# Three edits of order in a state-space and memory-attention kernel: V in four tiles, scalings before products on VectorE, the end of the third segment over more rounds

## The chip, the cores and the metric

The kernel runs on one core of one Trainium2 chip. That core has five engines that matter here: TensorE (PE in the profile, with its weight loads as PEld), VectorE (DVE), ScalarE (ACT), GpSimd (POOL) and SyncE (SP), which issues most of the DMAs. ScalarE and GpSimd also issue a few (ACTq, POOLq). The metric is device time in microseconds (us) from start to end of one launch; lower is better. The profile's own clock, the span, starts at the first recorded instruction.

## The reference

Two branches on the same input are mixed by a gate. `a` is a diagonal state-space layer, whose kernel `K` of length 2048 is built from exponentials and applied as a long convolution by FFT; `b` is attention in four segments of 512 tokens with a memory that is carried from segment to segment. Cut to what matters:

```python
# a: convolution through the spectra
P = exp((A * dt[:, None])[:, :, None] * pos)            # D=448, N=256, L=2048
K = 2.0 * einsum("dn,dnl->dl", C, P).real
y = irfft(rfft(u_t, 2 * L) * rfft(K, 2 * L))[..., :L] + u * D_skip
# b: 16 heads of 28, segments s = 0..3
for s in range(4):
    p = softmax(qs @ ks.T * scale + causal)
    a_dot = p @ vs
    a_mem = (phi(qs) @ M) / (phi(qs) @ z + 1e-6)
    outs.append(g * a_mem + (1 - g) * a_dot)
    M, z = M + phi(ks).T @ vs, z + phi(ks).sum()
b = concat(outs) @ wo
out = gate * a + (1 - gate) * b
```

## The kernel before

The program has a first half (to about 430 us) that builds `K`, transforms the input and projects Q, K and V into DRAM, and a second half, `second_half`, in which all the edits lie. There the work is written out by hand in **units** and **rounds**.

A unit `i` (0 to 15) is one group of four heads, `hg = i % 4`, of one segment, `s = i // 4`. It has six rounds `r` (0 to 5), and one pass of the loop in `second_half` issues one round of many generators, each of which goes on by one step:

- `pair`: the scores of unit `i` (`weigh`: matmuls into the bank `ps_w`, exponential on ScalarE into `PT`, the causal mask on GpSimd), interleaved with the row maxima of unit `i + 2` (`maxima`: mask matmuls and scores into `ps_mx`, then a maximum on VectorE into `mx`). `ps_w` and `ps_mx` have one buffer each, so a round's mask matmuls wait for the maximum of the round before.
- in rounds 0 and 1, the last steps of the maxima of unit `i + 1` (`peak`): a transpose into the bank `ps_m`, a copy `mn`, and a DMA from GpSimd's queue into the Q tile.
- in rounds 0, 1 and 2, `values` of the unit before: the product of `PT` and V into `ps_pv`, key tile 0 in round 0, key tile 1 in round 1, key tiles 2 and 3 and a copy to `pvs` in round 2. So unit 4's round 2 is the last use of segment 0's V, and unit 5's round 0 the first of segment 1's.
- a step of `seg_end`, the end of a segment, if one is under way (`ends`).
- a step of `convolve`: of 16 blocks of the spectra, in turn `transform` (kernel spectrum to `ks`, with a swap of halves by DMA), `product` (input spectrum, and two multiplications `pr` on VectorE), an empty step, and `back` (inverse matmuls into `ps_c`, first half with the first product, second half with the second; copy `bs`, stored to DRAM). It runs in units 1 to 12.

A round to which none of these brings matmuls (`busy` is false) is followed by two or three filler matmuls, `turn_over`.

The engines' orders are fixed: TensorE's and ScalarE's by the program's order, VectorE's in `attend` and `convolve` by `k.dve`, which chains each instruction to the one issued before. The two multiplications of a block are not issued where they arise. `product` puts them on the list `k.later`, and `catch_up` takes them from it: one behind each maximum (line 1053), up to two more after `peak` (line 1404), one at once in rounds 1 and 2 (`k.spread`), and the rest ahead of `back` (line 646). So they stand on VectorE ahead of whatever the segment's end issues in that round.

`seg_end(s)` (line 1221) begins in round 2 of unit 4s + 4 and takes one step to a round, unless the table `STEPS` (line 1460) says more. Its steps:

1. load of four rows of the skip input `xt`; DMA of the softmax denominators out of `pvs` into `dn`, from ScalarE's queue.
2. to 5. four steps `t`, in each of which the recall from memory that an earlier end has prepared (`recall`) scales one head group, `am[hg]`, by a matmul into `ps_m` and one VectorE instruction; in the third, the reciprocal of `dn` (`inverse`) on VectorE, in the fourth its two DMAs.
6. and 7. skip input times gate on ScalarE and times `D_skip` on GpSimd (`scaled`), two tiles a step.
8. to 11. `norm` scales one head group of `pvs` a step: a matmul into `ps_m` (for `s == 2` every second one into `ps_c`), one VectorE instruction, and for `s > 0` a second, which adds `am`.
12. to 19. the projection with `wo`, four tiles of two halves each (`out_mm`, "po"): two head groups to a half, all in `ps_m`; after the second half one VectorE instruction makes `tb`, which goes to DRAM (`TB`). The loads and the reciprocal of the next recall are issued in between.
20. to 23., for `s == 2` only: the four scalings of the last recall, all through `ps_m`.

`STEPS` gives the third segment's end 2, 3, 2 and 2 steps in rounds 2 to 5 of unit 13, and in unit 14 each round has two. `ps_m` has a single buffer, shared by transposes, scalings and projection.

In unit 14 round 2 `join` starts to load the `rest` tiles out of `TB`; from unit 14 round 4 `last` does the final transform of the convolution, in `ps_c` and `ps_mx` by turns, and adds `rest`. Its results go to `out` and, for the last segment, to `YD`, from which `last_end` (line 1270) reads them once more.

V of a segment is one tile, 128 x 4 x 512, with one buffer (`load_v`, line 1100). It is loaded in round 2 of units 4, 8 and 12 (line 1410), behind its last use.

Of the kernel before, what the change touches and what calls it, by code (L numbers as in the profile page):

```python
# [27 lines left out]
SEG = 512  # L28
# [955 lines left out]
def attend(nc, k, ap):  # L984
# [36 lines left out]
    def maxima(i):  # L1021


        q, kk = Q[i], K[i]
        mx = ap.tile([128, 4, 4], F32, tag="mx", name="mx", bufs=2)
        for b, hp in MSTEPS:
            pt = k.ps("mx")
            o, n = DIAGONALS[b]
            for j in range(4):
                for x in range(2):  # L1030
                    h = 2 * hp + x
                    r = slice(32 * h, 32 * h + 32)
                    k.mm(
                        pt[:, x, o : o + n].rearrange("p (b c) -> p b c", c=128)[:, :, 32 * j :],
                        k.mk[r, j, :128],
                        k.mk[r, j, 128 : 128 + n].rearrange("p (b c) -> p b c", c=128)[:, :, 32 * j :],
                        start=(j == 0), stop=True, tile_position=(32 * h, 0), skip_group_check=True,
                    )
            yield
            for t, o, n in PLACES[b]:  # L1040
                qt = 3 - t
                for x in range(2):
                    h = 2 * hp + x
                    r = slice(32 * h, 32 * h + 32)
                    k.mm(
                        pt[:, x, o : o + n], q[r, 0, 128 * qt : 128 * qt + 128], kk[r, 0, :n],
                        start=False, stop=True, tile_position=(32 * h, 0), skip_group_check=True,
                    )
            for t, o, n in PLACES[b]:
                v.tensor_reduce(  # L1050
                    mx[:, 2 * hp : 2 * hp + 2, 3 - t : 4 - t], pt[:, :, o : o + n], AX.X, ALU.max,
                )
            k.catch_up(1)
            yield
        yield
        yield
        pm = k.ps("m")
        k.tr(pm[:16, :128], mx.rearrange("p h t -> p (h t)"), k.ident)
        mn = ap.tile([16, 128], F32R, tag="mn", name="mn", bufs=2)
        act(mn, pm[:16, :128], AF.Copy, scale=-1.0)  # L1060
        k.pdma(
            q[:, 0].rearrange("(j e) (t c) -> e j t c", e=32, c=128)[28].bitcast(F32),
            mn.bitcast(F32),
        )
        yield
        yield
# [30 lines left out]
            ):  # L1097
                nc.gpsimd.affine_select(sl, sl, pat, ALU.is_ge, 0.0, base=0, channel_multiplier=-1)  # L1098

    def load_v(s):  # L1100
        Vs[s] = ap.tile([128, 4, SEG], F32, tag="V", name="V", bufs=1)
        k.dma(Vs[s], k.VD[SEG * s : SEG * s + SEG].rearrange("(t p) h e -> p t (h e)", p=128))

    def values(i):
        s, hg = divmod(i, 4)
        if hg == 0:
            pvss[s] = ap.tile([128, 4, SEG], F32, tag="pvs", name="pvs", bufs=2)
        yield
        V, pvs, PT = Vs[s], pvss[s], W.pop(i)
        pv = k.ps("pv")  # L1110
        for kt in range(4):
            if kt in (1, 2):
                yield
            o = (0, 512, 1024, 896)[kt]
            for h in range(4):
                k.mm(
                    pv[32 * h : 32 * h + 32, 128 * kt :],
                    V[:, kt, (4 * hg + h) * 32 : (4 * hg + h) * 32 + 32],
                    PT[:, h, o : o + SEG - 128 * kt],
                    start=(kt == 0), stop=(kt == 3), tile_position=(0, 32 * h),  # L1120
                )
        act(pvs[:, hg], pv, AF.Copy)
        yield
# [20 lines left out]
    def recall(s):  # L1144

        dn = ap.tile([128, 64], F32, tag="dm", name="dm", bufs=1)
        k.ldma(dn, k.DM[s - 1].rearrange("j h (i f) -> (j h i) f", f=64))
        yield
        am[s] = ap.tile([128, 4, SEG], F32, tag="am", name="am", bufs=1)
        k.ldma(am[s], k.AM[:, :, s - 1].rearrange("h p q -> p h q"))  # L1150
        yield
        v.tensor_scalar(dn, dn, 1e-6, None, ALU.add)
        yield from inverse(dn, 32, r8)
        yield
        for hg in range(4):
            pb = k.ps("m")
            k.mm(pb, k.sel[32:40], r8[32:40, hg], start=True, stop=True)
            v.scalar_tensor_tensor(am[s][:, hg], am[s][:, hg], k.gh[:, hg : hg + 1], pb, ALU.mult, ALU.mult)
            yield
# [28 lines left out]
    def scaled(s, t, xt):  # L1188

        i = 4 * s + t  # L1190
        act(xt, xt, AF.Copy, scale=k.gt[:, i : i + 1])
        k.pin(nc.gpsimd.tensor_tensor(xt, xt, k.dbc, ALU.mult))
# [28 lines left out]
    def seg_end(s):  # L1221
        xts = [skip(s, t) for t in range(4)]
        sums, memory = norm(s), recall(s + 1)
        recalled = old.pop() if old else iter(())
        old.append(memory)
        next(sums)
        yield
        for t in range(4):
            next(recalled, None)
            if t > 1:  # L1230
                next(sums)
            yield
        for t in range(0, 4, 2):
            scaled(s, t, xts[t])
            scaled(s, t + 1, xts[t + 1])
            yield
        next(memory)
        for _ in range(4):
            next(sums)
            yield  # L1240
        for t in range(4):
            if t < 3:
                next(memory)
            po = k.ps("m")
            out_mm(s, t, po[:, :D], range(2))
            half.append(s)
            yield "po"
            half.pop()
            out_mm(s, t, po[:, :D], range(2, 4))
            store(s, t, po[:, :D], xts[t])  # L1250
            yield "po"
        if s == 2:
            for _ in memory:
                yield
# [49 lines left out]
def second_half(nc, k, ap, tp, fp, fin):  # L1304
# [1 line left out]


    none = object()
    k.later = []

    def catch_up(n=2):
        for op in k.later[:n]:
# [62 lines left out]
    fp = fp()  # L1375
    cv = convolve(nc, k, fp)
    step(cv)
    k.load_v(0)
    vals = k.values(0)
    step(vals)  # L1380
    turn_over(3)
# [4 lines left out]
    for i in range(16):  # L1386
        if i > 0:
            k.load(i + 3)
        ahead = ms.get(i + 2, nothing)
        behind = ms.get(i + 1, nothing)  # L1390
        w = k.weigh(i)
        for r in range(6):
            if i == 0 or not busy:
                turn_over(3 if i == 0 or 0 < r < 5 else 2)
            pair(w, ahead)
            busy = False
            if r < 2:
                if r == 1 and k.half:
                    step(ends[0])
                peak(behind)  # L1400
            if i == 0 and r in (0, 2):
                turn_over(2)
                peak(behind)
            k.catch_up()
            k.spread = r in (1, 2)
            if i > 0 and r < 3:
                step(vals)
                busy = True
                if r == 2 and i % 4 == 0:
                    k.load_v(i // 4)  # L1410
                    ends.append(k.seg_end(i // 4 - 1))
            for _ in range(STEPS.get((i, r), 2 if i == 14 else 1)):
                x = next(ends[0], none) if ends else none
                if x is none:
                    ends = ends[1:]
                busy = busy or x == "po"
            if (i, r) in DIVIDE:
                if k.half:
                    step(ends[0])
                k.divide(DIVIDE[i, r])  # L1420
            if 1 <= i <= 12:
                x = next(cv, "rest")
                if x == "more":
                    step(cv)
                busy = busy or x != "rest"
            if (i, r) in SKIPS:
                step(skips)
            if i == 13 and r < 5:
                load_b(r)
            if i == 14 and r == 2:  # L1430
                for wc in range(6):
                    join(wc)
            if i == 14 and r >= 4 or i == 15:
                busy = True
                last(n)
                if n < 2:
                    join(n + 6)
                if n < 3:
                    load_b(n + 5)
                n += 1  # L1440
        step(w)
        if i == 1:
            k.load_wo()
        if i > 0:
            for _ in vals:
# [11 lines left out]


SKIPS = ((2, 0), (2, 4), (2, 5), (3, 0), (3, 1), (3, 2))
STEPS = {(13, 2): 2, (13, 3): 3, (13, 4): 2, (13, 5): 2}  # L1460
DIVIDE = {(14, 5): 0, (15, 2): 1, (15, 4): 2}


# [296 lines left out]
```

## Time and profile before

| what | us |
|---|---|
| median of 3 runs | 783.25 (783.14 to 785.11) |
| the profiled execution, its own time | 780.51 |
| its span | 778.7 |
| mean granted clock of TensorE | 0.967 of full |
| scores of unit 4, 5 and 6 begin (of the span) | 518.01, 533.10, 551.43 |
| of unit 8 and 9 | 595.27, 610.10 |
| of unit 12, 13, 14 and 15 | 674.03, 690.94, 712.45, 737.94 |

In the profile a line of the timeline has the start, the length, the engine, the line of the code, the operation, what it writes and reads, how many were merged, and in brackets the idle time of that engine just before and what ended it. Line 1476 and line 1522 are helpers through which nearly all instructions go, so the tiles' names tell them apart. A line of waits has total time, number and longest. A line of a table of windows has the stretch, its length, the busy time of TensorE, its weight loads, VectorE, ScalarE and GpSimd with counts, and at the end the granted clock, the share of the DMA engines' time, and GB/s.

### The profile page before, as it was taken

What the parts mean: (1) busy time and instruction counts of PE and PEld (TensorE: products, weight loads), DVE (VectorE), ACT (ScalarE), POOL (GpSimd) and SP (SyncE); (2) the same over time, 40 slices, a digit from 0 to 9 for tenths busy, and PEclk for the clock granted to TensorE, in tenths of its full rate; (3) what the DMA queues carried; (4) which work ended last, traced back from release to release, by engine and by line L of the source; (5) the groups of instructions that cost most, each with busy time, mean ns of one, the idle gap of its engine ahead of it and who ended that gap; (6) DMA issues with size and microseconds to landing.
All of it is one profiled execution on the core that took longest, in us unless ns stands there. A gap on an engine that the chain in (4) does not pass through costs nothing.

```text
span 778.7 us, 19775 instructions
## 1 busy us (share of the span) xinstructions
PE 681.5 (88%) x8273; PEld 371.0 (48%) x8289; DVE 560.4 (72%) x758; ACT 502.7 (65%) x621; POOL 157.9 (20%) x193
## 2 busy tenths in 40 slices
PE   1685998999988998889999999898899789979897
PEld 1362555666555665457664444343334334434333
DVE  8989679878899788888875345565555675674486
ACT  4877689889999989988986425665435353451220
POOL 5405300110111101110120002343311221132110
PEclk9998999999999999999999989999999899999899
DMA  9428774234563345733356797999676867556686
GB/s 242 127 71 247 231 250 131 70 106 161 156 219 111 108 126 168 231 130 105 117 211 237 283 323 274 324 333 338 230 233 207 305 208 244 195 195 242 171 266 191
DMA packets 91550, 158.00 MB, mean 203 GB/s; under 512 B 22174, under 2 KB 59542, under 8 KB 91462
## 3 DMA queue, kind: packets, MB, share of 16 engines
q1 hardware_dynamic: 85530, 153.55, 59.9%
q10 hardware_dynamic: 5052, 2.33, 1.2%
q8 instruction: 65, 1.06, 0.6%
q0 software_dynamic: 880, 0.87, 0.4%
q14 instruction: 23, 0.19, 0.1%
HBM read 88.51 MB, written 60.24 MB: 191 GB/s over the span
## 4 chain that ended last, share of the span: by engine, by line
PE 53%; ACT 18%; DVE 14%; DMA 8%; issue 4%; SPq 1%; POOL 1%; ACTq 0%; DVEq 0%; POOLq 0%
PE ps_m L1522 23%; PE ps_c L1522 8%; ACT cs L1476 6%; PE ps_w L1522 5%; PE ps_pv L1522 5%; PE ps_arg L1522 4%; PE ps_mx L1522 4%; PE ps_k L1522 4%; ACT EY L1476 2%; DVE pr L1476 2%; DVE mx L1476 2%; DMA WD<-wsp 1%; DVE xl L906 1%; ACT L1476 1%; DMA V<-VD 1%
## 5 line engine op out<-in xcount | busy, mean ns | idle before, releaser
L1476 DVE TENSOR_REDUCE mx<-ps_mx 128x2 f32<-128x1024 f32 (+3 forms) x128 | 102.4, 821 | 96.2 <-PE ps_mx L1522 93.1
L1476 ACT ACTIVATE PT<-ps_w 128x1024 f32<-128x1024 f32 (+1 forms) x96 | 84.5, 881 | 128.5 <-PE ps_w L1522 119.4
L366 POOL TENSOR_TENSOR EX<-EX,cab 128x1024 f32<-128x1024 f32 x28 | 53.5, 1913 | 288.2 <-ACT EX L1476 266.6
L1476 ACT ACTIVATE cs<-ps_arg 128x1024 f32<-128x1024 f32 x97 | 94.5, 1023 | 3.7 <-DVE Y L414 2.4
L1522 PE MATMUL ps_w<-qu,ku 32*128 32x512 f32 (+3 forms) x768 | 89.5, 350 | 4.6 <-ACT PT L1476 3.3
L1098 POOL TENSOR_SCALAR_AFFINE_SELECT PT<-PT 128x256 f32<-128x256 f32 (+1 forms) x96 | 47.4, 494 | 227.0 <-ACT PT L1476 219.6
L1522 PE MATMUL ps_m<-xh,w 112*128 112x512 f32 x256 | 91.4, 410 | 1.3 <-DMA w<-WD 1.3
L1522 PEld LDWEIGHTS ps_w<-qu,ku 32*128 32x128 f32 x768 | 58.6, 189 | 68.0 <-ACT PT L1476 30.7
L409 DVE TENSOR_TENSOR X<-EX,cs 128x1024 f32<-128x1024 f32 x56 | 69.3, 1238 | 12.6 <-ACT cs L1476 11.8
L1522 PE MATMUL ps_k<-Y,X 128*32 128x64 f32 x3584 | 64.1, 226 | 14.4 <-DVE Y L414 14.4
L1522 PEld LDWEIGHTS ps_k<-Y,X 128*32 128x32 f32 x3584 | 54.9, 113 | 40.4 <-DVE Y L414 22.4
L413 DVE TENSOR_TENSOR Y<-EY,cs 128x1024 f32<-128x1024 f32 x56 | 70.1, 1253 | 0.0
L1476 ACT ACTIVATE cs<-cs 128x1024 f32<-128x1024 f32 x56 | 59.2, 1057 | 1.3
L1522 PEld LDWEIGHTS ps_m<-xh,w 112*128 112x128 f32 x256 | 48.1, 188 | 21.1 <-issue 8.3
L1476 ACT ACTIVATE EY<-ps_arg 128x1024 f32<-128x1024 f32 x52 | 51.3, 1036 | 3.9 <-PE ps_arg L1522 3.7
L1522 PE MATMUL ps_arg<-ct,lh 64*128 64x512 bf16 x224 | 46.4, 384 | 7.0 <-ACT EY L1476 4.9
L1522 PE MATMUL ps_m<-xl,w 112*128 112x512 f32 x128 | 50.3, 393 | 0.0
L1522 PE MATMUL ps_pv<-PT,V 128*32 128x128 f32 (+3 forms) x512 | 46.4, 461 | 4.4 <-DMA V<-VD 4.4
L1522 PEld LDWEIGHTS <-lh 64*128 64x128 bf16 x392 | 20.2, 94 | 59.0 <-issue 46.5
L1522 PE MATMUL ps_m<-wo,pvs 128*128 128x448 f32 x96 | 43.9, 589 | 1.4 <-ACT mn L1476 1.1
L1522 PE MATMUL ps_mx<-ku,qu 32*128 32x512 f32 (+3 forms) x256 | 44.4, 379 | 0.3 <-DMA ku<-KD 0.3
L415 DVE SCALAR_TENSOR_TENSOR Y<-EY,cs 128x512 f32<-128x512 f32 x56 | 40.0, 715 | 3.8 <-ACT cs L1476 2.5
(219 smaller groups left out, 1284.0 us busy)
## 6 DMA issues: line engine op xcount, KB each, us to landing
w<-WD SPq DMA_DIRECT2D x32, 448.0 KB
qu<-QD SPq DMA_DIRECT2D x16, 512.0 KB
ku<-KD SPq DMA_DIRECT2D x16, 512.0 KB
GU<-gs SPq DMA_DIRECT2D x32, 224.0 KB
GK<-gs SPq DMA_DIRECT2D x8, 896.0 KB
gk<-GK SPq DMA_DIRECT2D x16, 448.0 KB
gu<-GU SPq DMA_DIRECT2D x16, 448.0 KB
ks<-ks SPq DMA_DIRECT2D x32, 224.0 KB
```

The costliest lines, as they stand in the source:

```text
L366: nc.gpsimd.tensor_tensor(o, o, cab, ALU.mult)
L409: v.tensor_tensor(X, ex, t[:, :, 0], ALU.mult)
L413: v.tensor_tensor(Y[:, :, :, :32], lo, y[:, :, :, ::-1], ALU.mult)
L415: v.scalar_tensor_tensor(Y[:, 1, :, 32:], ey[:, :, 32:], -1.0, y[:, 1], ALU.mult, ALU.mult)
L906: v.tensor_tensor(xl[:, :, ts_], pv, xh[:, :, ts_], ALU.subtract)
L1098: nc.gpsimd.affine_select(sl, sl, pat, ALU.is_ge, 0.0, base=0, channel_multiplier=-1)
L1476: x = op(*args, **kw)
L1522: tc.keep_in_program_order(nc.tensor.matmul(*args, **kw))
```

## The change

Three edits, all in `attend` and `second_half`.

V becomes four tiles, one for each key tile of 128 rows, each with a buffer of its own. After the step of `values` in rounds 0, 1 and 2 of units 4, 8 and 12 the tiles that this step used last are loaded anew: tile 0, tile 1, tiles 2 and 3. The first V is loaded by four DMAs in place of one.

A flag `k.scaling` is set by `seg_end` before a step that scales. While it is set, the maximum is not followed by a product, and the general `k.catch_up()` of a round moves from ahead of `values` and the segment's end to behind them. So where a product of the spectra and a scaling fall into one round, the scaling comes first.

In the end of the third segment the first two skip tiles are scaled one step earlier, together with the last recall step, which makes the end a step shorter, and `STEPS` keeps only the two steps of unit 13's round 5. The four scalings so fall to rounds 2, 3, 4 and 5 of unit 13, the first half of the projection to round 5, and the other seven halves to unit 14. The last recall uses `ps_c` for every second head group.

```diff
-            k.catch_up(1)
+            if not k.scaling:
+                k.catch_up(1)
...
-    def load_v(s):
-        Vs[s] = ap.tile([128, 4, SEG], F32, tag="V", name="V", bufs=1)
-        k.dma(Vs[s], k.VD[SEG * s : SEG * s + SEG].rearrange("(t p) h e -> p t (h e)", p=128))
+    def load_v(s, t):
+        Vs[s, t] = ap.tile([128, SEG], F32, tag=f"V{t}", name="V", bufs=1)
+        o = SEG * s + 128 * t
+        k.dma(Vs[s, t], k.VD[o : o + 128].rearrange("p h e -> p (h e)"))
...
-                    V[:, kt, (4 * hg + h) * 32 : (4 * hg + h) * 32 + 32],
+                    Vs[s, kt][:, (4 * hg + h) * 32 : (4 * hg + h) * 32 + 32],
...
-            pb = k.ps("m")
+            pb = k.ps("c")[:, 0] if s == 3 and hg % 2 else k.ps("m")
...
         next(sums)
+        k.scaling = s > 0
         yield
         for t in range(4):
             next(recalled, None)
             if t > 1:
                 next(sums)
+            if s == 2 and t == 3:
+                scaled(s, 0, xts[0])
+                scaled(s, 1, xts[1])
+            k.scaling = s > 0 and t < 3
             yield
-        for t in range(0, 4, 2):
+        for t in range(2 if s == 2 else 0, 4, 2):
             scaled(s, t, xts[t])
             scaled(s, t + 1, xts[t + 1])
+            k.scaling = t == 2
             yield
         next(memory)
-        for _ in range(4):
+        for hg in range(4):
             next(sums)
+            k.scaling = hg < 3
             yield
...
-    k.load_v(0)
+    for t in range(4):
+        k.load_v(0, t)
...
-            k.catch_up()
             k.spread = r in (1, 2)
             if i > 0 and r < 3:
                 step(vals)
                 busy = True
+                if i % 4 == 0:
+                    for t in ((0,), (1,), (2, 3))[r]:
+                        k.load_v(i // 4, t)
                 if r == 2 and i % 4 == 0:
-                    k.load_v(i // 4)
                     ends.append(k.seg_end(i // 4 - 1))
...
+            k.catch_up()
             if (i, r) in DIVIDE:
...
-STEPS = {(13, 2): 2, (13, 3): 3, (13, 4): 2, (13, 5): 2}
+STEPS = {(13, 5): 2}
```

More of the change, by code (lines that the diff above doesn't have):

```diff
@@ L1108, in values @@
         yield
-        V, pvs, PT = Vs[s], pvss[s], W.pop(i)
+        pvs, PT = pvss[s], W.pop(i)
         pv = k.ps("pv")
@@ L1308, in second_half @@
     none = object()
-    k.later = []
+    k.later, k.scaling = [], False
     def catch_up(n=2):
```

## The prediction

> **What bounds the kernel now.** I read the page first, then TensorE's waits in the second half (from 430 us, where attention, inverse transform and projection run), then the clock in stretches of 2 us, and last the timeline around each long wait.
>
> ```profile
> PE 681.5 (88%) x8273; PEld 371.0 (48%) x8289; DVE 560.4 (72%) x758; ACT 502.7 (65%) x621; POOL 157.9 (20%) x193
> ...
> PE ps_pv L1522 <- DMA V<-VD: 4.4, 2, 2.6
> PE ps_m L1522 <- DVE am L1476: 4.0, 4, 2.0
> ...
> PE ps_c L1522 <- DVE pvs L1476: 2.1, 1, 2.1
> ...
> PE ps_m L1525 <- DVE pvs L1476: 1.6, 1, 1.6
> ```
>
> TensorE is the bound at 88%, and its longest waits in this half are those that the change goes for: the reload of V, and the scalings `am` and `pvs`, which hold the only `ps_m` bank. Each costs more than itself:
>
> ```profile
> 536.00:538.00 2.00, 2.00 (x12) 0.33 (x11) 1.47 (x3) 0.00 (x0) 0.00 (x0) 0.50 1.01 402
> 538.00:540.00 2.00, 2.00 (x24) 0.52 (x16) 0.00 (x0) 0.48 (x1) 0.00 (x0) 0.65 0.60 207
> ...
> 558.00:560.00 2.00, 2.00 (x3) 0.93 (x4) 0.00 (x0) 0.00 (x0) 0.00 (x0) 0.53 1.01 373
> ...
> 690.00:692.00 2.00, 2.00 (x24) 0.89 (x16) 0.40 (x2) 0.92 (x1) 0.00 (x0) 0.50 0.00 0
> ```
>
> The third number from the right is the granted clock. Right behind each long wait it is half: 0.50 and 0.65 over 4 us of busy TensorE lose 1.0 + 0.7 = **1.7 us**, which I take for each such drop.
>
> **The change, part by part.** V first, at unit 5 round 0 (segment 1's first use of V):
>
> ```profile
> 534.00:536.00 2.00, 0.21 (x6) 0.16 (x8) 0.65 (x2) 1.18 (x2) 0.41 (x1) 1.00 1.06 374
> ...
> 527.16 0.55 SPq L1538 DMA_DIRECT2D V<-VD  x1
> ...
> 535.32 0.55 DVE L1476 RECIPROCAL rc<-dn 128x64 f32<-128x64 f32 x1 [2.41 <-DMA dn<-pvs]
> ...
> 535.87 1.88 PE L1522 MATMUL ps_pv<-PT,V 128*32 128x512 f32 x8 [1.79 <-DMA V<-VD]
> ...
> 536.28 1.22 DVE L1476 TENSOR_REDUCE mx<-ps_mx 128x2 f32<-128x1024 f32 x1
> ...
> 539.39 0.32 PE L1522 MATMUL ps_mx<-mk 32*128 32x128 bf16 x8
> ```
>
> V is issued as a whole at 527.16 and holds TensorE from 534.08 to 535.87, with the DMA engines full (1.06). In tiles, the first goes two rounds earlier, and the last two are needed two rounds later; this wait goes. What is late next: VectorE sits behind the denominators `dn` until 535.32, so round 0's maximum ends at 536.28 + 1.22 = 537.5, and round 1's mask matmuls need it. The work from 535.87 to 539.39 (3.5 us at half clock) takes about 1.8 at full, so TensorE is there at 535.9 and waits to 537.5: 539.39 - 537.55 = **1.8 us** won, not the 1.79 + 1.7 that the wait costs. Bounds: 0 (`dn` later still) to 3.5 (`dn` early). I take the middle, as the total of bytes is the same and `dn` has no reason to move. [...]
>
> Scaling ahead of the products alters the order in four rounds only, as the generators step: unit 6 round 0, unit 9 rounds 0 and 5, unit 12 round 4. Elsewhere no product is pending beside a scaling. Unit 6 round 0:
>
> ```profile
> 553.32 0.49 PE L1522 MATMUL ps_m<-r,sel 8*128 8x512 f32 x1
> ...
> 553.37 2.08 DVE L1476 TENSOR_TENSOR pr<-ps_c,ks 128x896 f32<-128x896 f32 x2
> ...
> 555.36 0.74 DVE L1476 SCALAR_TENSOR_TENSOR pvs<-pvs,omg,ps_m 128x512 f32<-128x512 f32 x1
> ...
> 556.15 0.28 PE L1525 MATMUL ps_m<-ident,mx 128*16 128x128 f32 x1 [1.62 <-DVE pvs L1476]
> ...
> 561.42 0.45 PE L1522 MATMUL ps_mx<-mk 32*128 32x256 bf16 x8
> ```
>
> The scaling can start at 553.32 + 0.49 = 553.8 and free `ps_m` at 554.6: the transpose goes 1.5 earlier, and the drop behind it (0.53) goes too: 1.7. The two products then end at 556.7, the next maximum (1.22) at 557.9; round 2's mask comes at 561.42 - 3.2 = 558.2, so both are just in time: **3.2 us**. Bounds 0 to 3.3 (wait and drop).
>
> Unit 9 round 0 has both edits:
>
> ```profile
> 613.15 0.55 DVE L1476 RECIPROCAL rc<-dn 128x64 f32<-128x64 f32 x1 [3.14 <-DMA dn<-pvs]
> ...
> 613.68 1.18 PE L1522 MATMUL ps_pv<-PT,V 128*32 128x512 f32 x8 [2.61 <-DMA V<-VD]
> ...
> 614.11 1.22 DVE L1476 TENSOR_REDUCE mx<-ps_mx 128x2 f32<-128x1024 f32 x1
> ...
> 617.24 0.74 DVE L1476 SCALAR_TENSOR_TENSOR am<-am,gh,ps_m 128x512 f32<-128x512 f32 x1
> ...
> 618.04 0.38 PE L1525 MATMUL ps_m<-ident,mx 128*16 128x128 f32 x1 [1.40 <-DVE am L1476]
> ...
> 621.45 0.45 PE L1522 MATMUL ps_mx<-mk 32*128 32x256 bf16 x8
> ```
>
> With `dn` unmoved the maximum still ends at 615.33, so the 2.61 us is a wait for `dn` instead of V, and the clock falls as before. `am` then ends at 616.1 instead of 617.98; the transpose comes at 616.6, 1.4 earlier, and the rest follows: **1.4 us**, between 0 and 2.61 + 1.40 + 1.7 = 5.7. Unit 9 round 5 swaps scaling and products before a matmul that needs both: nothing, within 0.3 either way.
>
> Unit 12 round 4:
>
> ```profile
> 684.81 0.69 DVE L1476 TENSOR_REDUCE mx<-ps_mx 128x2 f32<-128x512 f32 x1 [0.28 <-PE ps_mx L1522]
> ...
> 685.42 2.08 DVE L1476 TENSOR_TENSOR pr<-ps_c,ks 128x896 f32<-128x896 f32 x2
> ...
> 687.41 0.74 DVE L1476 SCALAR_TENSOR_TENSOR am<-am,gh,ps_m 128x512 f32<-128x512 f32 x1
> ...
> 688.20 0.50 PE L1522 MATMUL ps_m<-r,sel 8*128 8x512 f32 x1 [2.04 <-DVE am L1476]
> ...
> 688.63 2.38 PE L1522 MATMUL ps_c<-pr,cb 64*64 64x448 f32 x16
> ```
>
> `am` first: 685.5 to 686.25, products at 687.3 and 688.35. The inverse's halves start at 687.4 and 688.4 and end near 689.4 instead of 691.0: 1.6, and with the clock up (0.50 at 690) I add 0.4, no more, as VectorE is then back to back: **2.0 us**, 0 to 3.7.
>
> The third segment's end, units 13 and 14:
>
> ```profile
> 701.77 0.49 PE L1522 MATMUL ps_c<-r,sel 8*128 8x512 f32 x1 [2.11 <-DVE pvs L1476]
> ...
> 703.66 4.75 PE L1522 MATMUL ps_m<-wo,pvs 128*128 128x448 f32 x8
> ...
> 709.25 2.15 PE L1522 MATMUL ps_m<-wo,pvs 128*128 128x448 f32 x5 [0.30 <-DVE tb L1476]
> ...
> 719.80 3.27 PE L1522 MATMUL ps_m<-wo,pvs 128*128 128x448 f32 x8 [0.27 <-ACT mn L1476]
> ...
> 725.93 1.11 SPq L1538 DMA_DIRECT2D rest<-TB  x2
> ...
> 728.00:730.00 2.00, 1.16 (x3) 0.42 (x3) 0.82 (x2) 0.28 (x1) 0.41 (x1) 0.50 1.04 269
> 730.00:732.00 2.00, 1.78 (x8) 0.86 (x7) 0.67 (x1) 0.00 (x0) 0.00 (x0) 0.50 1.05 238
> 732.00:734.00 2.00, 2.00 (x9) 0.77 (x8) 0.00 (x0) 0.60 (x1) 0.64 (x1) 0.51 1.05 238
> ```
>
> What goes: three scalings in one round (2.11) and the drop behind it (4.75 instead of 3.27 for eight projection matmuls: 1.5); the last recall's four matmuls on one bank (4.0 in the waits, less unit 12's 2.04: 1.9) and its drop (half of 1.16, 1.78 and 2.00: 2.4). Together 7.9. What comes: one scaling to a round makes VectorE the slower one in unit 13 rounds 3 and 4, about 1.0 of waits (maximum and scaling against pair and filler); one more filler pair, 0.5; in unit 14 a tile's first half now follows directly on the half before, which holds the one `ps_m`: 709.25 - (703.66 + 4.75) = 0.84, twice; the recall's last scaling now shares its round and the `ps_c` bank with the final transform's first block, 1.1. Together 4.3, so 3.6 won on TensorE. I take off 1.6 by choice, not the whole, as the stores of the last rows of this segment move one round back, into the one in which the `rest` loads start (725.93), and behind these stand the last loads of the kernel: **2.0 us**, between -4 and 7.9.
>
> Twelve more V issues cost SP some 0.5 us each (527.16), hidden in its waits. Each now waits on SP for one tile's matmuls, and the swaps of `ks` and the spectra stand behind it; these are used a block, four to five rounds, later. The two skip scalings that move a round ahead are hidden on ScalarE, which waits for scores there; else 0.6 each.
>
> Sum: 1.8 + 3.2 + 1.4 + 2.0 + 2.0 = **10.4 us**. The profiled execution took 780.5 (span 778.7), so 770.1; the median of the runs is 783.25, 2.7 higher, so **772.9**.
>
> **The rivals.**
> *`dn` and VectorE take over* (0.15): the early V tiles put more bytes ahead of `dn` in a DMA system that is already full (1.06), VectorE waits longer, and the V edits (1.8 and 1.4) and half of unit 12 give nothing: 6.2 won, 777. For it: both reciprocals wait (2.41, 3.14).
> *`dn` lands 2 us earlier* (0.10), as only half of V is in its way: then unit 5 gains its full 3.5 and unit 9 some 4: 14.7 won, 768.5. Against it: the bytes stay the same.
> *Given back at the end* (0.10): V gives nothing, and the three new waits of units 14 each drop the clock (1.7 each, 5.1): 3.2 + 2.0 + 2.0 - 5.1 = 2.1 won, 781. For it: the clock fell behind a wait of 1.62; against it: these are shorter. [...]
> *Slower* (0.07): unit 13's rounds don't get shorter when the projections leave them, since VectorE or the exponentials hold them. Then seven half projections (0.41 x 4 each, 11.5) stand in unit 14 instead of four (6.5), the `rest` loads come 5 later plus the three waits (2.8), and the end with them: +7.8. It decides where V, units 6 and 12 win less than that; with 4 of the 8.4, 787. Against it: nothing in round 3 of unit 13 but the 2.11 wait is long.
>
> **How the numbers follow.** Forecast 0.58 at 772.9. The range takes in the first two rivals: 767.5 to 780.5, 0.83. A measurement tells about 0.3% (2.4 us) from no change: faster 0.83, same 0.10, slower 0.07.
>
> **What would show it.** Right: no wait for V; the waits of `ps_m` for `am` and `pvs` under 1 us; clock 1.00 near units 5, 6 and 13; the reciprocals of `dn` still waiting; unit 13 shorter by about 6, unit 14 longer by about 3. Wrong: TensorE waiting for `pr` or `mx` as long as it did for V; half clock at the same places; the last `rest` results waiting for a DMA.

## The result and the profile after

The changed kernel took 789.79 us in the median of 20 runs (783.70 to 823.74), the kernel before 783.26 beside it (20 runs). The ratio is **1.0099, 95% interval 1.0075 to 1.0124**: about 1% slower, where 1.3% faster was forecast. The profiled execution took 791.54 with a span of 789.8, which is 11.1 more than before's 778.7. (Medians are of all runs here and below; the ratios leave out the runs in a slower state, of the changed kernel those of 796.90 and 823.74.)

The page's first line of engines and, in TensorE's waits from 420 us to the end (total, number, longest), the three that stand where those shown of before stood:

```profile
PE 687.7 (87%) x8291; PEld 373.2 (47%) x8291; DVE 560.6 (71%) x758; ACT 503.3 (64%) x621; POOL 156.9 (20%) x193
```

```profile
PE ps_w L1534 <- ACT PT L1488: 10.2, 13, 3.8
PE ps_mx L1534 <- DMA bt<-BB: 6.8, 1, 6.8
...
PE ps_c L1534 <- DVE am L1488: 1.3, 1, 1.3
```

The waits that the change went for are gone: none for V, none of `ps_m` for `am` or `pvs` longer than 0.3. Two new ones stand in their place, one for the exponentials `PT` and one for the load `bt` of the final transform. Two others grew: for `pr` from 1.5 to 4.8 in total, for `mx` from 1.6 to 3.2. VectorE, which was to go on waiting for `dn`, no longer waits for it (5.5 before). (Lines 1488, 1534 and 1550 are 1476, 1522 and 1538 of before.)

Where the time went is best read by stages. ScalarE runs one exponential per round, 96 in all, and its start marks the round. The table has the time from one mark to another, in us, worked out from ScalarE's timeline (5.1 is unit 5 round 1). Each column is one execution. The first two are before and after; the others are experiments told of below: S the scalings alone (the second of two runs), V the tiles alone, T the third segment's end alone, and the changed kernel with `dn` from GpSimd (D), with `bt` ahead on SP (B), with both (DB), and with `dn` from GpSimd and the old third end (DO).

| stage | before | after | S | V | T | D | B | DB | DO |
|---|---|---|---|---|---|---|---|---|---|
| 0.0 to 1.0 | 16.53 | 18.01 | 16.60 | 18.07 | 16.43 | 16.59 | 18.07 | 18.03 | 16.25 |
| 4.2 to 5.0 | 8.57 | **14.18** | 8.58 | 11.82 | 8.56 | 8.58 | 11.49 | 8.57 | 8.57 |
| 5.0 to 5.1 | 6.23 | 2.74 | 4.22 | 2.75 | 3.98 | 2.82 | 2.75 | 2.84 | 2.84 |
| 5.1 to 6.1 | 14.18 | 14.18 | 14.20 | 14.19 | 14.19 | 14.78 | 14.18 | 14.80 | 18.37 |
| 6.1 to 6.2 | 7.94 | 4.95 | 4.95 | 7.94 | 7.85 | 4.95 | 4.95 | 4.96 | 4.96 |
| 8.2 to 9.0 | 9.18 | **14.75** | 9.77 | 14.35 | 10.02 | 9.30 | 14.03 | 9.29 | 9.30 |
| 9.0 to 10.1 | 25.94 | 21.32 | 24.50 | 20.21 | 24.23 | 22.06 | 21.33 | 21.79 | 21.09 |
| 12.5 to 13.0 | 6.47 | 4.71 | 4.73 | 5.14 | 5.15 | 5.84 | 4.72 | 4.44 | 5.96 |
| 13.0 to 13.5 | 16.31 | 12.15 | 19.47 | 19.34 | 12.69 | 12.52 | 12.16 | 11.90 | 16.20 |
| 13.5 to 15.0 | 30.01 | **36.16** | 29.75 | 29.73 | 34.58 | 34.56 | 36.15 | 36.14 | 29.86 |
| 15.5 to the end | 21.92 | **31.17** | 21.92 | 22.20 | 32.67 | 32.42 | 22.22 | 24.06 | 22.44 |

The stages left out differ by less than 0.1, and mark 0.0 stands at 460.1 both before and after. After minus before: +1.5, +5.6, -3.5, 0, -3.0, +5.6, -4.6, -1.8, -4.2, +6.1, +9.3, together 11.0. So the change wins 17 in five places and loses 28 in five others.

The timeline of ScalarE and its DMA queue, before and after, in units 4 and 8. First before:

```profile
526.52 0.59 ACT L1476 ACTIVATE pvs<-ps_pv 128x512 f32<-128x512 f32 x1
527.44 1.11 ACTq L1165 DMA_DIRECT2D dn<-pvs  x1
528.60 1.02 ACT L1476 ACTIVATE PT<-ps_w 128x1024 f32<-128x1024 f32 x1 [1.49 <-PE ps_w L1522]
...
602.91 0.59 ACT L1476 ACTIVATE pvs<-ps_pv 128x512 f32<-128x512 f32 x1
604.67 0.57 ACTq L1165 DMA_DIRECT2D dn<-pvs  x1
605.29 1.02 ACT L1476 ACTIVATE PT<-ps_w 128x1024 f32<-128x1024 f32 x1 [1.79 <-DMA ks<-ks]
```

And after:

```profile
528.01 0.59 ACT L1488 ACTIVATE pvs<-ps_pv 128x512 f32<-128x512 f32 x1
532.03 1.11 ACTq L1167 DMA_DIRECT2D dn<-pvs  x1
533.19 1.02 ACT L1488 ACTIVATE PT<-ps_w 128x1024 f32<-128x1024 f32 x1 [4.58 <-issue]
...
603.53 0.59 ACT L1488 ACTIVATE pvs<-ps_pv 128x512 f32<-128x512 f32 x1
607.94 0.57 ACTq L1167 DMA_DIRECT2D dn<-pvs  x1
608.56 1.02 ACT L1488 ACTIVATE PT<-ps_w 128x1024 f32<-128x1024 f32 x1 [4.44 <-DMA gu<-GU]
```

`dn` can be gathered out of `pvs` as soon as that is copied. Before, its issue follows 0.3 later in unit 4 and 1.2 later in unit 8. After, `pvs` is ready at 528.60 and 604.12, but the issue comes 3.4 and 3.8 later, and the exponential of round 3, which stands behind it in ScalarE's order, is held with it. The "issue" and the "DMA gu" that the brackets name are two names for that hold. ScalarE's idle time is 3.1 and 2.7 longer than before (4.58 against 1.49, 4.44 against 1.79); the rest of the 5.6 in each unit I put down to the clock, which is half for 6.8 and 10.2 us there instead of 3.4 and 6.8. TensorE waits 3.8 for `PT`, and the clock falls, as the windows of the changed kernel show (clock, DMA share and GB/s last):

```profile
530.00:534.00 4.00, 0.51 (x3) 0.01 (x1) 2.16 (x3) 0.81 (x1) 0.00 (x0) 1.00 1.05 407
534.00:538.00 4.00, 3.73 (x44) 1.89 (x48) 0.89 (x2) 0.85 (x3) 1.04 (x2) 0.52 0.58 202
538.00:542.00 4.00, 4.00 (x32) 1.20 (x32) 2.67 (x5) 2.20 (x3) 0.64 (x1) 0.62 0.75 282
```

Why the issue waits can be read from the two traces, which hold for each DMA the counter on which its arrivals are booked. SP's and ScalarE's DMAs share eight, in turn over both queues: behind 430 us, 246 of 259 successive issues before and 259 of 273 after step to the next counter (the others stand around ScalarE's DMAs `r`). And none of the 260 DMAs before and the 274 after is issued ahead of the last arrival of the one before it on its counter, eight places back where the turn is kept; 22 and 30 of them follow that arrival within 0.1 us. Around `dn` in unit 4 (counter in brackets):

```
before:  qu(3) ku(4) cb(5) BB(6) gk(7) ks(0) ks(1) V(2)              dn(3) waits for qu
after:   cb(1) BB(2) V tile 1(3) gk(4) ks(5) ks(6) V tile 2(7) V tile 3(0)   dn(1) waits for cb
```

In unit 8 it was a swap of `ks` and is `gu`. The arrivals on the counters of `dn` are such close ones: the last part of `cb` arrives at 531.95 and `dn` is issued at 532.03; `gu` at 607.86 and `dn` at 607.94; before, `qu` at 527.37 and `dn` at 527.44. SP's timeline has `qu` issued 7.2 ahead of `dn` before, and `cb` 7.0 ahead of it after, where `dn` was ready 3.6 behind `cb`:

```profile
520.29 0.36 SPq L1538 DMA_DIRECT2D qu<-QD  x1
```

```profile
525.04 0.33 SPq L1550 DMA_DIRECT2D cb<-in_c_bk  x1
```

How much a hold costs differs by execution. In V alone, B and the third end undone `dn` waits for the same transfers; there unit 4 (4.2 to 5.0) lost 2.9 to 3.9 and unit 8 (8.2 to 9.0) 3.8 to 5.2 instead of 5.6, and in unit 4 the half clock lasted 3.4 us instead of 6.8.

The end, in the timeline of SP. Before:

```profile
725.93 7.50 SPq L1538 DMA_DIRECT2D rest<-TB  x12
734.79 0.55 SPq L1538 DMA_DIRECT2D bt<-BB  x1
736.10 0.80 SPq L1538 DMA_DIRECT2D YD<-rest  x2
...
745.84 0.55 SPq L1538 DMA_DIRECT2D bt<-BB  x1
...
754.87 1.09 SPq L1538 DMA_DIRECT2D rest<-TB  x2
```

After:

```profile
729.81 7.51 SPq L1550 DMA_DIRECT2D rest<-TB  x12
737.42 1.74 SPq L1550 DMA_DIRECT2D YD<-rest  x2
739.21 1.99 SPq L1550 DMA_DIRECT2D out<-rest  x2
741.89 0.56 SPq L1550 DMA_DIRECT2D bt<-BB  x1
...
754.92 1.72 SPq L1550 DMA_DIRECT2D rest<-TB  x2
756.68 0.58 SPq L1550 DMA_DIRECT2D out<-rest  x1
757.31 0.55 SPq L1550 DMA_DIRECT2D bt<-BB  x1
```

SP's order is fixed when the program is built, by the times expected then. With the `rest` loads four later, the stores of block 0 went ahead of the load of block 5, and the load of block 7, the last, fell behind `rest` 7, which waits for a buffer whose stores must end: 757.31 instead of 745.84. TensorE's timeline and a window show what that costs (the 6.83 are idle time, and the clock is half behind it):

```profile
765.42 1.01 PE L1534 MATMUL ps_mx<-bt,fc 128*64 128x448 f32 x2 [6.83 <-DMA bt<-BB]
```

```profile
764.00:768.00 4.00, 2.58 (x8) 0.86 (x8) 0.30 (x1) 0.00 (x0) 0.00 (x0) 0.50 0.80 253
```

### The profile page after: what moved, and what is told of

Its sections match the earlier page's. It is cut to its first block, busy times and chain, and to the rows that moved or that the text cites. A ratio compares the mean times of both kernels' runs of the same rounds, so it can differ in the third digit from the quotient of the medians.

```text
span 789.8 us, 19827 instructions
## 1 busy us (share of the span) xinstructions
PE 687.7 (87%) x8291; PEld 373.2 (47%) x8291; DVE 560.6 (71%) x758; ACT 503.3 (64%) x621; POOL 156.9 (20%) x193
## 4 chain that ended last, share of the span: by engine, by line
PE 54%; ACT 17%; DVE 13%; DMA 9%; issue 4%; SPq 2%; POOL 1%; ACTq 0%; DVEq 0%; POOLq 0%
PE ps_m L1534 21%; PE ps_c L1534 9%; PE ps_w L1534 6%; ACT cs L1488 5%; PE ps_pv L1534 5%; PE ps_mx L1534 5%; PE ps_arg L1534 4%; PE ps_k L1534 3%; ACT EY L1488 2%; DVE pr L1488 2%; DVE mx L1488 2%; DMA WD<-wsp 1%; DVE pvs L1488 1%; ACT PT L1488 1%; ACT L1488 1%
## 5 line engine op out<-in xcount | busy, mean ns | idle before, releaser
L1534 PE MATMUL ps_w<-qu,ku 32*128 32x512 f32 (+3 forms) x768 | 92.3, 357 | 10.4 <-ACT PT L1488 10.2
L1534 PEld LDWEIGHTS ps_w<-qu,ku 32*128 32x128 f32 x768 | 60.7, 195 | 76.4 <-ACT PT L1488 41.8
```

The costliest lines, as they stand in the source:

```text
L1534: tc.keep_in_program_order(nc.tensor.matmul(*args, **kw))
```

## The experiments

Theory: V's tiles shift the completion counters, so that `dn` holds ScalarE; and the new third end reorders the last loads on SP. Rivals: the tiles' bytes make `dn` late, whoever issues it; the scalings' order is to blame; the end is late because the `rest` loads are.

### The three parts, one at a time

**The third end undone** (the other two parts stay):

```diff
-            if s == 2 and t == 3:
-                scaled(s, 0, xts[0])
-                scaled(s, 1, xts[1])
...
-            pb = k.ps("c")[:, 0] if s == 3 and hg % 2 else k.ps("m")
+            pb = k.ps("m")
...
-STEPS = {(13, 5): 2}
+STEPS = {(13, 2): 2, (13, 3): 3, (13, 4): 2, (13, 5): 2}
```

> The changed kernel with its third part undone: the third segment's end is stepped, scaled and recalled as before; V in tiles and the scalings ahead of the products stay. Theory (last loads): in the changed kernel the later rest loads let the stores of the first joined blocks go ahead of the loads bt 5 to 7 on SP, and the last of these lands at 765.4; here the wait of 6.8 us for it is gone and so is the half clock behind it, and units 13 and 14 lose their 2: 9 to 11 us less than the changed kernel, ratio to before 0.995 to 1.000. Rival (third part good, the loss is all in units 0 to 8): the end is 0 to 2 us longer than the changed kernel's, as the three scalings in a row stand again, ratio 1.010 to 1.013.

Measured: 780.51 us, ratio to before 0.9976 (0.9948 to 1.0003), 1.2% below the changed kernel. The wait for `bt` is gone, and the stage to the end is 22.24. The theory holds.

**The scalings alone** (V whole, old third end):

```diff
-            k.catch_up(1)
+            if not k.scaling:
+                k.catch_up(1)
...
-            k.catch_up()
             k.spread = r in (1, 2)
...
+            k.catch_up()
             if (i, r) in DIVIDE:
```

> The kernel before with one part of the change, the scalings ahead of the products; V is loaded whole and the third segment's end is as before. Theory: this part is innocent and worth what was forecast for units 6, 9 and 12: 3.2 + 0 to 1.4 + 2.0, so 4 to 6.5 us less than before, ratio 0.992 to 0.995, with the half clock at 538 and 613 still there. Rival (moving the products later makes TensorE wait for pr): no gain or up to 2 us slower, 0.999 to 1.003.

Measured: 778.77 us, ratio 0.9909 (0.9856 to 0.9963), a little better than the theory's range. This part is innocent of the loss. Its stage 6.1 to 6.2 is 4.95 instead of 7.94. The rival's mechanism is there but does not outweigh it: TensorE's waits for `pr` are 4.2 in total, in every kernel with the scalings ahead 4.2 to 5.2, in the others 1.1 to 1.6. The profile also has a loss of 2.7 in unit 13, which has a cause of its own (last section).

**V in tiles alone** (the diff's `load_v`, `values` and their calls, on the kernel before):

> The kernel before with one part of the change, V in four tiles. Theory (completion lanes): ScalarE's DMA of dn waits, as the program is built, for the DMA eight places before it over both queues, which is now the load of cb issued 2 us before it; ScalarE stands 3 to 5 us in units 4 and 8, about as much as the waits for V were worth, and unit 0 loses 1.5 to the longer half clock: 0 to 4 us slower than before, ratio 1.000 to 1.005; the longest waits are ScalarE's exponentials behind the issue of dn and TensorE's for them. Rival (tiles work, the loss is elsewhere): no such wait, 2 to 6 us faster, 0.992 to 0.997.

Measured: 783.38 us, ratio 1.0008 (0.9978 to 1.0038), as the theory had it: 2.75 in stage 5.0 to 5.1 with the wait for V gone, and the hold in units 4 and 8 (stages of 11.82 and 14.35). In ScalarE's timeline, unit 4:

```profile
532.91 1.02 ACT L1484 ACTIVATE PT<-ps_w 128x1024 f32<-128x1024 f32 x1 [3.68 <-issue]
```

**The third end alone** (V whole, products ahead):

> The kernel before with the third part of the change alone; V whole, products ahead of scalings. Theory: units 13 and 14 together change by -2 to +2, then the last loads are reordered on SP as in the changed kernel and the end costs 8 to 10 more: ratio 1.009 to 1.014, with a wait for bt of 6 to 8 us near the end. Rival (the flip on SP needs the other parts too): no such wait, 0.996 to 1.002.

Measured: 791.40 us, ratio 1.0113 (1.0072 to 1.0154). Units 13 and 14 together, 13.0 to 15.0, are 47.3 against 46.3, and the end is 10.8 longer, in TensorE's timeline:

```profile
763.76 1.01 PE L1529 MATMUL ps_mx<-bt,fc 128*64 128x448 f32 x2 [9.08 <-DMA bt<-BB]
```

The reordering needs no other part.

### `dn` from another queue

One edit to the changed kernel:

```diff
-        k.pin(k.adma(
+        k.pin(k.pdma(
             dn,
```

> The changed kernel with one edit: the DMA that gathers dn is issued from GpSimd, not from ScalarE. Same bytes at the same place in the order. Theory (completion lanes): the wait for the load eight places before no longer stands in ScalarE's stream; the exponentials of unit 4 rounds 3 to 5 and unit 8 rounds 3 to 5 are not held (their waits of 4.6 and 4.4 gone), and what remains is at most a wait of VectorE for dn: 5 to 8 us less than the changed kernel, ratio to before 0.999 to 1.004. Rival (the DMA engines are full, dn itself is late whoever issues it): dn still lands after 536, the loss only moves from ScalarE to VectorE, 0 to 2 us less, 1.007 to 1.010.

Measured: 786.22 us, ratio 1.0050 (1.0008 to 1.0092), 3.6 below the changed kernel by the medians, which is less than the 5 to 8 expected, and 7.0 by the profiled executions. (`dn` also leaves the row of eight, as none of GpSimd's 23 DMAs in the trace of the changed kernel is booked on these; so the counters behind it shift by one place.) ScalarE's timeline in unit 4:

```profile
530.96 1.02 ACT L1488 ACTIVATE PT<-ps_w 128x1024 f32<-128x1024 f32 x1 [1.19 <-PE ps_w L1534]
```

The hold is gone, both stages are back at 8.58 and 9.30, and the wait for V stays away: unit 10 begins 8.4 earlier than in the changed kernel. VectorE waits only 0.2 for `dn`. The same bytes are loaded in the same order, so the rival of bytes falls.

**Four tiles, loaded at once.** To tell counters from early loads in the other direction, V in four tiles on the kernel before, all issued where the whole V was:

```diff
-                    for t in ((0,), (1,), (2, 3))[r]:
+                    for t in ((), (), (3, 0, 1, 2))[r]:
                         k.load_v(i // 4, t)
```

This is the difference from V alone; besides, tiles 0 to 2 are tied behind tile 3 on SP.

> The kernel before with V in four tiles, but all four loaded together where the whole V was loaded: the same bytes at the same place, only four DMAs instead of one. In the program as built, the DMA of dn now waits for ku (512 KB, the load behind qu) in unit 4 and for gu in unit 8; in the kernel before it waited for qu and for ks. Theory (a DMA waits for the one eight places before it, over both queues): in unit 4 the hold of ScalarE is short, under 2 us, as ku lands at most 1.3 us behind the point where dn was issued before; in unit 8 it is 3 to 4.5 us, as with the early tiles, the exponential of round 3 late by that. Rival (early V tiles put bytes ahead of dn): no hold in either unit, as in the kernel before.

Measured: 780.70 us in its one run, the kernel before 780.05 beside it. In ScalarE's timeline:

```profile
530.27 1.11 ACTq L1170 DMA_DIRECT2D dn<-pvs  x1
531.43 1.02 ACT L1488 ACTIVATE PT<-ps_w 128x1024 f32<-128x1024 f32 x1 [3.24 <-issue]
...
606.53 0.57 ACTq L1170 DMA_DIRECT2D dn<-pvs  x1
607.15 1.02 ACT L1488 ACTIVATE PT<-ps_w 128x1024 f32<-128x1024 f32 x1 [3.42 <-DMA gu<-GU]
```

This execution ran 1.08 and 0.23 behind that of before when these stretches began. So `dn` goes out 1.75 late in unit 4, as the theory had it, and 1.6 late in unit 8, where the idle time is within the 3 to 4.5 expected, but 1.79 of it was there before. The arrivals fit again: `ku` at 530.20 and `dn` at 530.27, `gu` at 606.45 and `dn` at 606.53. With the bytes in their old place there is a hold all the same: the place in the row of counters makes it, not only when the tiles start. The two stages are 11.76 and 13.48, near those of V alone (11.82 and 14.35).

### The order on SP

One edit to the changed kernel, the load of block n + 5 ahead of the stores of block n:

```diff
-    def last(wc):
+    def last(wc, after):
...
+        x = load(after) if after else None
         yo = rest.pop(wc)
...
         for h in range(2):
-            k.dma(yv[h, :, ws], yo[64 * h + 48 : 64 * h + 64])
+            with k.issue_after(x.ins) if x and not h else ExitStack():
+                nc.sync.dma_start(yv[h, :, ws], yo[64 * h + 48 : 64 * h + 64])
...
-                last(n)
+                last(n, n + 5 if n < 3 else 0)
...
-                if n < 3:
-                    load_b(n + 5)
```

> The changed kernel with one edit: in the final transform the load of block n+5 (bt) is put ahead of the stores of block n on SP, so that bt 7 no longer stands behind the load rest 7, which waits for the stores of block 1 to end. Nothing else moves; the rest loads start as late as in the changed kernel. Theory (order on SP): bt 7 goes out some 7 to 9 us earlier against its round, TensorE's wait of 6.8 us for it falls under 2, the half clock behind it goes, the time from unit 15 round 5 to the end is 22 to 25 us instead of 31: 6 to 9 less than the changed kernel, ratio to before 0.998 to 1.003. Rival (the end is late because the rest loads start late and the DMA engines are full): the wait only moves to the rest results or to the stores, 0 to 2 less.

Measured: 781.83 us, ratio 0.9985 (0.9953 to 1.0018), some 8 below the changed kernel. The `rest` loads begin as late against the rounds as there, no wait for `bt` is left, and the end is 22.22. In SP's timeline `bt` 7 is ahead of `rest` 7:

```profile
747.37 0.61 SPq L1550 DMA_DIRECT2D bt<-BB  x1
748.08 1.02 SPq L718 DMA_DIRECT2D YD<-rest  x2
749.62 1.09 SPq L1550 DMA_DIRECT2D rest<-TB  x2
```

It is the order, not the late `rest` loads.

### Both mended, and what is left

**`dn` from GpSimd and the third end as before:**

> V in tiles and the scalings ahead of the products as changed, dn gathered from GpSimd, and the third segment's end as before. If the two causes are what the first runs say (ScalarE held behind the issue of dn: some 8 us by unit 10; bt 7 late on SP: some 9 us at the end), both are gone here and the first two parts of the change give what was forecast for them, 1.8 + 3.2 + 1.4 + 2.0 = 8.4, or more where dn no longer lands late: 7 to 11 us less than before, ratio 0.986 to 0.991. Rival (the two losses are not independent, VectorE takes over where ScalarE is freed): 2 to 5 less, 0.994 to 0.997.

Measured: 777.24 us, ratio 0.9908 (0.9876 to 0.9940), in the range of the theory. (The same kernel, run again below, was outside it.)

**`dn` from GpSimd, `bt` ahead, the new third end:**

> The whole change with both mends: dn gathered from GpSimd, bt n+5 ahead of the stores of block n on SP. It tells what the third part is worth once the last loads stand right, beside the run that has the third segment's end as before. Theory: units 13 and 14 are 0 to 2 us longer with the new end (waits for tb, am and the half clock behind them against the wait for pvs), so this is 0 to 3 slower than that run and 6 to 9 less than before, ratio 0.988 to 0.993. Rival (the forecast of 2.0 won there was right and only the last loads spoiled it): 2 faster than that run, 0.984 to 0.988.

Measured: 777.73 us, ratio 0.9923 (0.9882 to 0.9963), the same within the intervals. So with both mends the change does beat the kernel before, by less than 1%. The new third end neither helps nor harms that one can tell from the times; in the profiles DB and DO it is 2.0 longer in units 13 and 14 and 1.6 at the end.

**The same, with the last recall on one bank:**

```diff
-            pb = k.ps("c")[:, 0] if s == 3 and hg % 2 else k.ps("m")
+            pb = k.ps("m")
```

> The whole change with both mends (dn from GpSimd, bt ahead of the stores), less the second bank in the last recall: its four scalings all use ps_m again. It splits the 6.1 us by which unit 14 grew. Theory (the wait of 1.27 us for am on the bank that the first joined block needs drops the clock over the blocks behind it): without it the half clock around the first blocks of unit 14 round 4 is gone or shorter, and unit 14 is 1 to 3 us shorter than in the run with both mends. Rival (the waits for tb and the work moved in make up the 6.1; waits for am on ps_m come back): unit 14 is 0 to 2 us longer.

Measured, in one run of 778.44 us (before 780.05): unit 14 is 4.6 longer (13.5 to 15.0 is 40.76 instead of 36.14). Of it 2.5 come before the recall's first scaling, in rounds where the two programs do the same and the clock is half for longer; 2.1 come behind. The theory falls. The rival had the direction, and its 0 to 2 fits the 2.1. But programs that are alike differ by as much in such stages, so one execution doesn't show that the second bank is worth having; it shows that the half clock doesn't hang on that one wait.

**The best two side by side**, `dn` from GpSimd with the old third end, and the scalings alone:

> The same kernel as the run with dn from GpSimd and the third segment's end as before (V in tiles, scalings ahead), now side by side with the scalings alone, to see what V in tiles is worth once dn no longer holds ScalarE. By the lengths of the stages in the profiles so far (unit 5 round 0 some 1 to 2 shorter than in the kernels with V whole, units 8 and 9 some 3 shorter) it should be 4 to 6 us below the scalings alone and 8 to 10 below before, ratio 0.987 to 0.991. Rival (V in tiles gives nothing that lasts): the two are within 1.5 us of each other.

> The scalings ahead of the products alone, on the same chip: unit 6 is 3.0 shorter and the rest as before, so 3 to 5 us less than before, ratio 0.994 to 0.997, unless the end of the third segment again loses 2 to 3 where VectorE's addition of am meets GpSimd's product of the inputs; rival (V in tiles gives nothing): 0.987 to 0.991 as the other.

Measured: 776.47 us, ratio 0.9947 (0.9915 to 0.9979), and 778.70, ratio 0.9949 (0.9916 to 0.9981). The 2.2 between the medians can't be told from nothing, and by the ratios the two are equal: the theory's 4 to 6 did not come, and V in tiles is not shown to give anything that lasts. Both kernels had been run before with 0.9908 and 0.9909, so 0.4% between two series of runs is within what happens. The profile of the first says where the tiles' gain can go once `dn` is early: to the next step of the same chain, the DMAs `r` behind the reciprocal, in TensorE's timeline

```profile
544.14 0.46 PE L1531 MATMUL ps_m<-r,sel 8*128 8x512 f32 x1 [2.57 <-DMA r<-rs]
```

with a clock of 0.59 in the 4 us from 544; its stage 5.1 to 6.1 takes 18.37 instead of 14.18. The run with the recall on one bank has the same wait (1.66) and 19.06 there; D and DB wait 0.4 and take 14.8. So it comes in some executions and not in others; how often stays open.

## Why the prediction was wrong

**V, forecast 1.8 in unit 5 and 1.4 with `am` in unit 9: measured 2.1 lost in units 4 and 5, 1.0 lost in units 8 to 10.** The wait went, and what it gave was not too small: 5.0 to 5.1 is 2.7 to 2.8 in the table's kernels with tiles, 4.0 to 6.2 in those with V whole, and 8.2 to 10.1 falls from 35.1 to 31.1 once `dn` comes from GpSimd. The step that failed is "`dn` has no reason to move", and with it "twelve more V issues cost SP some 0.5 us each (527.16), hidden in its waits". I priced a DMA by its issue and its bytes. Its place in the row of eight counters was the price: 5.6 us in each of two units here, 2.9 to 5.2 in the other kernels with tiles and `dn` on ScalarE. The first rival (`dn` late) had the mark but not the engine: it had VectorE wait for `dn`, and it was ScalarE that waited to issue it. The second rival's sizes, 3.5 and some 4 with `dn` early, are about what the mended kernels show in these stages, but part is given back behind them (5.1 to 6.1), and the total shows no gain.

**Unit 6, forecast 3.2: measured 3.0**, in every kernel of the table with this edit and in none without it. (V in four at once, without the edit, took 6.29 instead of 7.94, as the clock stayed up there: the half clock in this term can stay away by itself.) VectorE's timeline of the changed kernel has the scaling first, and TensorE's wait for it is 0.20 instead of 1.62:

```profile
557.54 0.75 DVE L1488 SCALAR_TENSOR_TENSOR pvs<-pvs,omg,ps_m 128x512 f32<-128x512 f32 x1 [0.48 <-PE ps_m L1534]
```

```profile
558.34 0.28 PE L1537 MATMUL ps_m<-ident,mx 128*16 128x128 f32 x1 [0.20 <-DVE pvs L1488]
```

**Unit 12, forecast 2.0: measured 1.8, but not shown.** Kernels without the edit take 5.1 to 6.8 in this stage (the high one is V in four at once), kernels with it 4.4 to 6.9 (the third end undone): executions differ by more than the term. In the changed kernel TensorE waits 1.51 for `pr` there, where it waited 2.04 for `am`.

**The third segment's end, forecast 2.0 won: 11.3 lost**, of this 2.0 in units 13 and 14 and 9.3 at the end. In unit 13 the mechanism was right, 4.2 won where about 6 was expected; unit 14 lost 6.1 where about 3 was. The waits came as forecast (0.83 twice for `tb`, 1.26 for `am`). What failed is the term for the clock: I booked the half clock behind the old waits, 1.5 and 2.4, as won, because no new wait is as long as those behind which the clock fell. The windows of the changed kernel show that it fell all the same:

```profile
700.00:704.00 4.00, 2.37 (x23) 0.92 (x22) 3.97 (x7) 1.25 (x2) 2.10 (x4) 1.00 1.03 413
704.00:708.00 4.00, 3.93 (x21) 1.56 (x20) 3.31 (x6) 0.60 (x1) 0.64 (x2) 0.61 1.04 409
...
728.00:732.00 4.00, 2.74 (x18) 1.30 (x17) 2.81 (x4) 1.62 (x2) 1.04 (x2) 1.00 0.36 117
732.00:736.00 4.00, 4.00 (x15) 1.60 (x12) 1.28 (x2) 0.58 (x1) 0.00 (x0) 0.52 1.03 248
736.00:740.00 4.00, 4.00 (x12) 0.97 (x12) 2.44 (x3) 0.02 (x1) 0.64 (x1) 0.63 1.04 238
```

TensorE is busy for 2.37 and 2.74 of 4 us, idle in pieces of at most 1.26, and half clock follows: 0.39 x 3.93 = 1.5 lost in unit 13, 0.48 x 4 + 0.37 x 4 = 3.4 in unit 14. So the 3.9 that I took as won stayed, and 1 more came: nearly all of the 5.6 between forecast (3.6 won on TensorE) and measurement (2.0 lost). This is read from the windows and not shown by a run: only the one-bank run tried it, and there the clock fell all the same. The rival "given back at the end" was near: of its three new waits the one for `am` was followed by half clock, for 6.8 us, the two for `tb` were not. For the `rest` loads and what stands behind them I took off 1.6 "by choice". The place was right and the mechanism wrong: not that they start later, but that the order on SP turned over, 9 to 11 in every kernel with the new end and without the mend.

**Slower**, at 0.07, had the third end lose because unit 13's rounds would not get shorter. They did. The outcome was on that side by two mechanisms that no case had, the hold of ScalarE and the order on SP.

## What to carry to other kernels

In a program built like this one, one more DMA moves the completion counter of every DMA behind it: here `dn` came from behind `qu` to behind `cb`, and its issue from 0.3 to 3.4 behind the copy `pvs`. So for each DMA that a compute engine issues, look at the one before it on its counter, here eight places back over two queues, and at when that one lands; the engine's own work stands behind it (ScalarE's idle time ahead of the next exponential was 4.58 instead of 1.49). Where a builder orders a DMA queue by expected times, compare the orders of both programs before costing a delay: what falls behind a load that waits for a buffer waits with it (`bt` 7, issued at 757.31 instead of 745.84). And don't book a clock drop as won because its one long wait is split: idle pieces of 0.64 and 0.34 were followed by half clock here, one of 1.51 by full clock (below).

## What the runs showed of the hardware

The clock of TensorE changed only at steps of 3.41 us: in the profiles of before and after, each of the 40 stretches of full or half clock between the first change and the last is a whole number of these steps long. In the changed kernel it is half from 704.86 to 708.27 and from 732.16 to 738.99. How long TensorE idled in the step before did not settle what followed. Two steps of the changed kernel:

```profile
687.79:691.21 3.42, 1.89 (x17) 0.69 (x17) 3.42 (x5) 0.60 (x1) 0.64 (x1) 1.00 0.01 2
701.45:704.86 3.41, 2.43 (x35) 1.26 (x34) 3.34 (x7) 0.77 (x2) 0.65 (x2) 1.00 1.02 407
```

The first, with one idle piece of 1.51, was followed by full clock, the second, with 0.98 of idle time in all, by half clock. In the profiles of before and after, from 430 us on, full clock gave way to half after every step in which TensorE was busy for less than 0.55 of it, and after none in which it was busy for more than 0.76; between them both came.

VectorE's addition of `am`, 0.69 where it is shortest, took four times that in some kernels, in the scalings alone for one. VectorE's timeline there, and GpSimd's:

```profile
696.08 2.96 DVE L1481 TENSOR_TENSOR pvs<-pvs,am 128x512 f32<-128x512 f32 x1
```

```profile
696.28 2.21 POOL L1193 TENSOR_TENSOR xt<-xt,dbc 128x448 f32<-128x448 f32 x2
```

It ends 0.55 behind GpSimd's two products, so most of a usual 0.69 would fit behind them. VectorE had started 0.20 ahead of GpSimd, and still it was VectorE's instruction that took longer: the two products took 2.21, and the two before them, at 693.68, took 2.25. The same end shows elsewhere: before, the second addition (701.75, 1.12) ends 0.55 behind two products (700.11, 2.21), and in the changed kernel the first (699.42, 1.42) ends 0.56 behind two (698.05, 2.23). What holds VectorE no run shows. The long addition came in both runs of the scalings alone (2.96 and 3.10), where the stage 13.0 to 13.5 took 19.05 and 19.47; before and in DO, where the first addition took 0.72 and 0.83, it took 16.31 and 16.20. In the runs of the scalings alone the addition starts 0.20 and 0.34 ahead of GpSimd's products, before 0.96 ahead: less than a microsecond between the two engines goes with some 3 in the stage.

Programs that are alike up to a point differed in stages where the clock is about to fall: 5.0 to 5.1 with V whole took 6.23, 4.22 and 3.98 (before, S and T). So with unit 0, where the changed kernel loses 1.5: it took 18.0 to 18.1 in four of the table's six kernels with V in tiles and 16.2 to 16.6 in two, 16.4 to 16.6 in the three with V whole and 17.8 in the first run of the scalings alone. The changed kernel has three steps of half clock there, before, S and T have two. Whether the four first loads make the longer case likelier stays open. A term of that size in such a stage needs more than one profile.
